# Scores and y on four 64x64 TensorE tiles from chunk 3 on, in a windowed attention followed by a maxout FFN

## Chip, cores and metric

The kernel runs on one core of one Trainium2 chip. The metric is the device time of one execution in microseconds. Engines: TensorE (PE, with its weight loads as PEld), VectorE (DVE), ScalarE (ACT), GpSimd (POOL), and SyncE (SP), which here only issues DMAs.

## The reference

Attention with a causal window of 128 keys and 4 sink keys that every query sees, over 4 batches, 8 heads, 768 positions and head size 64; its output, with heads side by side, goes through a feed-forward layer that takes the largest of three projections (512 to 768) and projects back.

```python
scores = scale * np.matmul(q, k.transpose(0, 1, 3, 2))
is_sink = pos[None, :] < n_sink
in_window = (rel >= 0) & (rel < window)      # rel = query position - key position
scores = np.where(is_sink | in_window, scores, -1e9)
a = softmax(scores)
x = np.matmul(a, v)                          # then (B*S, H*D) = (3072, 512)
h = np.maximum(np.maximum(x @ w1, x @ w2), x @ w3)
out = h @ w_out
```

Inputs and output are float32; the kernel multiplies in bfloat16 and sums in float32.

## The kernel before

The 3072 rows are cut into 12 chunks of 256, three per batch (CPB = 3). A chunk has two blocks of 128 positions, and position 2p+i of the chunk is stored as partition p with i beside it, so a block is 64 partitions by i = 0, 1. Chunks pass through stages whose order is written out by hand for every engine (`manual_schedule`): a long list for chunks 0 to 3 (L486 to L692), then a loop over i = 3..11 (L693) in which chunk n = i + 1 does its attention, chunk i the first FFN product and chunk m = i - 1 the second.

- `load` (L76) issues the DMAs of q, k and v from SP. Some are gated by a small POOL instruction that writes into their target first (L469, L473), which sets when SP may issue them.
- `cast_qk` (L95) and `cast_v` (L104) cast to bfloat16, in the loop on POOL: two casts for k, two for q, four for v (64 partitions each, into `vb`).
- q and k are transposed to head size by position (`qT`, `kT`): for early chunks on TensorE (`turn`, L109, `turn2`), from chunk 4 on by DMA transposes that SP issues (`turn_dma`, L150): one DMA for q, two for k (64 source partitions each).
- `sink_k`, `sink_v` (L224, L310), once per batch: POOL copies the sink keys out of `kT` to `ks`; TensorE picks the sink values with the selector `sel` into `sv`, DVE casts them to `vs`.
- `score` (L259): for a pair p of heads, head a sits in row half a of TensorE (64 rows each). The keys of a block are the stationary operand, 64x128, so two tiles, one per head, run side by side. Each head's 128x512 PSUM bank `st` takes [last block of the chunk before x first query block | own first block x both | own second block x second]. The first chunk of a batch leaves out the first part (128x384).
- `expo` (L282), ACT: exponential from PSUM to `e_sb`. `mask` (L289), DVE: product with a 0/1 mask `msk` (or `msk0` in a batch's first chunk, which lets the sink keys through). The masks are made at the start (`masks`, `factors`).
- `sink_score` (L294): scores against the sink keys, four column tiles of 128x32 (`sk`), and their exponential.
- `av_open`, `av` (L324, L339): product with v; a column of ones gives the sum, and DVE divides (`rc`, `x_sb`).
- `xpose_dma` (L375), SP: a DMA transpose of x to `xT`.
- `ffn_h` (L383): three products per pair of output blocks (864 matmuls of 128x256 in all); ACT copies the first from PSUM, DVE takes the maximum with the others.
- y = h @ w_out: for chunks 4 to 10 of the loop in `y_turn` (L422), two turns of twelve 64x128 matmuls between the score groups. In turn 0, row half a of the contraction adds to bank a, in turn 1 to the other, so the two row halves never write one bank together; a small matmul, the fence, guards the bank. Else `ffn_y` (L406) with full tiles.

The PSUM has eight banks, which the program hands out by a list (`bank`, `give`). In a pass i of the loop between the first and the last two, TensorE's order is: sink scores, scores of pairs 0 and 3, y turn 0, scores of pairs 1 and 2, y turn 1, `av_open`, `av` between groups of `ffn_h`. SP's order in a pass is: q transpose of chunk i+2, loads of chunk i+3, k transposes of chunk i+2, x transpose of chunk i+1, store of chunk i-1.

Of the kernel before, what the change touches and what calls it, by code (L numbers as in the profile page):

```python
# [16 lines left out]
def kernel(  # L17
# [31 lines left out]
    with tc.manual_schedule():  # L49
# [16 lines left out]

        RING = 4
# [6 lines left out]
        raws, bfs = {}, {}  # L74

# [28 lines left out]
        def cast_v(ci, n, i, eng):  # L104
            eng.tensor_copy(  # L105
                vb[ci % RING][64 * i:64 * i + 64, n, :, 0:D],
                raws[ci, "v"][64 * n:64 * n + 64, :, i])

        def turn(ci, w, g, eng=None):  # L109
# [8 lines left out]
            if w == "q":  # L118
                f(  # L119
                    qT[ci % RING][:, 2 * g:2 * g + 2].rearrange("q p i n r -> q (p i) (n r)"), pt)  # L120
            else:
# [28 lines left out]
        def turn_dma(ci, w):  # L150
# [7 lines left out]
            for n in range(2):  # L158
                nc.sync.dma_start_transpose(
                    out=kT[ci % RING][:, n].rearrange("q p i r -> q (p i) r"),  # L160
                    in_=bfs[ci, w][64 * n:64 * n + 64].rearrange("q p i a d -> q (p i a d)"))
# [27 lines left out]
        msk0 = const.tile([128, 2, 3, 128], BF16, name="msk0")  # L189

# [20 lines left out]

        sel = const.tile([128, 2, 32], BF16, name="sel")

# [10 lines left out]
        def sink_k(b):  # L224
            x = kT[(b * CPB) % RING]
# [33 lines left out]
        def score(ci, pairs):  # L259
            b, c = divmod(ci, CPB)  # L260
# [20 lines left out]

        def expo(ci, p):  # L282
            lo = 0 if ci % CPB else 1
# [5 lines left out]
        def mask(ci, p, eng=None):  # L289
            lo = 0 if ci % CPB else 1  # L290
# [3 lines left out]
        def sink_score(ci):  # L294
# [4 lines left out]
            for p in range(NP):  # L299
                nc.tensor.matmul(  # L300
                    st[32 * p:32 * p + 32].rearrange("q n (i r) -> q n i r", i=2),
                    lhsT=ks[b % 2][:, p],
                    rhs=qT[ci % RING][:, p].rearrange("q i n r -> q n i r"),
                    start=True, stop=True, tile_position=(0, 32 * p))
# [5 lines left out]
        def sink_v(b):  # L310
# [3 lines left out]
            for a in range(2):  # L314
                for p in range(NP):
                    nc.tensor.matmul(
                        sv[32 * p:32 * p + 32, a], lhsT=sel[:, a], rhs=x[:, 0, 2 * p + a],
# [21 lines left out]
        def av(ci, p):  # L339
# [16 lines left out]
            if ci not in xs:  # L356
                xs[ci] = work.tile([128, 2, NP, 2, D], BF16, tag="x", bufs=2, name="x_sb")
            nc.vector.tensor_mul(xs[ci][:, :, p], o[:, :, :, 0:D],  # L358
# [5 lines left out]
        def xpose(ci, t, eng=None):  # L364
            eng = eng or nc.scalar
            if t == 0:
                xTs[ci] = work.tile([128, 2, DS, 128], BF16, tag="xT", bufs=3, name="xT")
            pt = bank([128, DS, 128], BF16, "xt")
            x = xs[ci][:, t].rearrange("q p a d -> q (p a d)")
            for ds in range(DS):  # L370
                nc.tensor.transpose(pt[:, ds], x[:, ds * 128:(ds + 1) * 128], ident)
            (nc.scalar.copy if eng is nc.scalar else eng.tensor_copy)(xTs[ci][:, t], pt)
            give(pt)

        def xpose_dma(ci, eng=None):  # L375
            xTs[ci] = work.tile([128, 2, DS, 128], BF16, tag="xT", bufs=3, name="xT")
            (eng or nc.sync).dma_start_transpose(
                out=xTs[ci].rearrange("q t s r -> q (t s) r"),
                in_=xs[ci].rearrange("q t p a d -> q (t p a d)"))
# [3 lines left out]
        def ffn_h(ci, fp, wi, cuts=1, eng=nc.scalar):  # L383
# [3 lines left out]
            for f in range(2):  # L387
                c0 = (2 * fp + f) * 128
                for ds in range(DS):
                    nc.tensor.matmul(  # L390
                        hp[:, f].rearrange("q (i t r) -> q i t r", i=2, t=2),
                        lhsT=w_sb[wi][:, ds, c0:c0 + 128],
                        rhs=xTs[ci][:, :, ds].rearrange("q t (i r) -> q i t r", i=2),
# [28 lines left out]
        def y_turn(ci, turn):  # L422
# [3 lines left out]

            for fb in range(FB):
                for a in range(2):
                    t = a ^ turn
                    hp = slice(64 * a, 64 * a + 64)  # L430
                    nc.tensor.matmul(  # L431
# [420 lines left out]
```

## Time and profile before

| | |
|---|---|
| median of 3 runs | 177.1 us (176.81 to 177.53) |
| the profiled execution | 178.83 us, of which the span of its instructions 177.1 us |
| TensorE clock granted | 1.00 |
| DMA | 34.91 MB, mean 197 GB/s |

The span is counted from the first instruction of the program to the last. Rows of the timeline give start and length in us, the engine, the line of the kernel, the operation with its output and inputs, the tile of TensorE (contraction rows * output columns), the shape, and how many instructions are merged. A matmul's length contains its way through the array, so what a matmul costs in a stream is the distance between starts. Rows grouped by line give the busy time and the mean length in ns, then the idle time just ahead and what ended it. Rows of SPq are DMA issues; their length is SP's time, and the data land later.

### The profile page before, as it was taken

To read this page: it belongs to the slowest core of one execution; us is meant where nothing else is said; L and a number is where in the kernel's file an instruction comes from. 1 tells how busy PE (TensorE), PEld (TensorE's weight loads), DVE (VectorE), ACT (ScalarE), POOL (GpSimd) and SP (SyncE) were. 2 spreads that over 40 slices of the span, in tenths; PEclk is the share of its full clock that TensorE was granted. 3 is DMA by queue.
4 is the path that set the end of the run, shared out by engine and by line. 5 is a ranking of instruction groups with operands and counts; after the bars stand their busy time and mean duration, and the time that the engine had idled before them with its cause. 6 is when DMAs were issued, how large, how long until landed. Compare 5 with 4: busy or idle time off the path is not lost.

```text
span 177.1 us, 4816 instructions
## 1 busy us (share of the span) xinstructions
PE 167.9 (95%) x1956; PEld 128.2 (72%) x1961; DVE 121.7 (69%) x263; ACT 86.8 (49%) x174; POOL 65.9 (37%) x126
## 2 busy tenths in 40 slices
PE   7869988899999999999999999999999999999992
PEld 2436777676688588598698797697797796796871
DVE  3287763679599696677776775876776776876451
ACT  4588525477871931931823914914715716420210
POOL 7289605454685296056055046065073000000000
PEclk9999999999999999999999999999999999999999
DMA  5999999999999999799998999997999405303203
GB/s 144 298 282 181 161 223 236 222 288 276 277 197 302 289 229 237 172 301 171 229 262 214 230 217 234 183 273 194 255 210 226 73 15 162 122 0 63 118 2 118
DMA packets 70694, 34.91 MB, mean 197 GB/s; under 512 B 26640, under 2 KB 69136, under 8 KB 70672
## 3 DMA queue, kind: packets, MB, share of 16 engines
q1 hardware_dynamic: 64976, 31.33, 79.4%
q0 software_dynamic: 5552, 3.15, 12.9%
q8 instruction: 15, 0.25, 0.6%
q10 hardware_dynamic: 144, 0.13, 0.2%
q14 instruction: 7, 0.06, 0.1%
HBM read 25.17 MB, written 6.29 MB: 178 GB/s over the span
## 4 chain that ended last, share of the span: by engine, by line
PE 75%; DMA 11%; POOL 6%; DVE 5%; issue 2%; POOLq 0%; SPq 0%; DVEq 0%
PE h_ps L390 44%; PE y_ps L431 10%; DMA q_raw<-in_q_dram 7%; PE y_ps L411 6%; PE st L274 5%; PE o L350 5%; DMA v_raw<-in_v_dram 3%; POOL w L237 3%; DVE h_sb L401 2%; POOL vb L105 1%; PE o L332 1%; DVE e_sb L292 1%; PE y_ps L453 1%; DVE x_sb L358 1%; PE pt L115 1%
## 5 line engine op out<-in xcount | busy, mean ns | idle before, releaser
L390 PE MATMUL h_ps<-xT,w 128*128 128x256 bf16 x864 | 101.6, 273 | 0.9 <-DMA w<-in_moe_w_dram 0.8
L390 PEld LDWEIGHTS <-w 128*128 128x128 bf16 x864 | 81.6, 98 | 11.8 <-DMA w<-in_moe_w_dram 1.2
L401 DVE TENSOR_TENSOR h_sb<-h_sb,h_ps 128x512 bf16<-128x512 bf16 (+1 forms) x74 | 49.1, 670 | 19.7 <-PE h_ps L390 18.0
L286 ACT ACTIVATE e_sb<-st 128x512 bf16<-128x512 f32 (+1 forms) x96 | 45.9, 585 | 6.6 <-PE st L274 6.5
L397 ACT CAST h_sb<-h_ps 128x512 bf16<-128x512 f32 x35 | 20.6, 589 | 49.7 <-PE h_ps L390 49.6
L292 DVE TENSOR_TENSOR e_sb<-e_sb,msk 128x1024 bf16<-128x1024 bf16 (+1 forms) x42 | 28.0, 679 | 10.8 <-ACT e_sb L286 10.8
L105 POOL CAST vb<-v_raw 64x512 bf16<-64x512 f32 x42 | 27.8, 661 | 15.7 <-DMA v_raw<-in_v_dram 13.2
L101 POOL CAST k_bf<-k_raw 128x512 bf16<-128x512 f32 x18 | 11.0, 630 | 40.0 <-DMA k_raw<-in_k_dram 32.8
L358 DVE TENSOR_TENSOR x_sb<-o,rc 128x256 bf16<-128x256 f32 x48 | 20.4, 424 | 1.6
L431 PE MATMUL y_ps<-wo,h_sb 64*128 64x512 bf16 x168 | 20.7, 376 | 0.0
L350 PE MATMUL o<-vb,e_sb 128*128 128x65 bf16 x352 | 16.6, 193 | 0.8 <-ACT e_sb L286 0.8
L350 PEld LDWEIGHTS <-e_sb 128*128 128x128 bf16 x352 | 14.6, 97 | 3.2 <-ACT e_sb L286 1.0
L274 PE MATMUL st<-qT,kT 64*128 64x128 bf16 (+1 forms) x256 | 14.8, 237 | 0.2 <-DVE qT L119 0.2
L101 POOL CAST q_bf<-q_raw 128x512 bf16<-128x512 f32 x17 | 10.2, 619 | 9.0 <-DMA q_raw<-in_q_dram 9.0
L274 PEld LDWEIGHTS <-kT 64*128 64x128 bf16 x256 | 9.2, 94 | 5.6 <-issue 1.8
L431 PEld LDWEIGHTS <-h_sb 64*128 64x128 bf16 x168 | 8.9, 94 | 5.7
L411 PE MATMUL y_ps<-wo,h_sb 128*128 128x512 bf16 x49 | 12.6, 380 | 0.3
L355 DVE RECIPROCAL rc<-o 128x4 f32<-128x4 f32 x48 | 8.4, 174 | 3.6 <-PE o L350 3.6
L306 ACT ACTIVATE e_sink<-sk 128x256 bf16<-128x256 f32 x8 | 3.1, 389 | 13.3 <-PE sk L300 13.3
L411 PEld LDWEIGHTS <-h_sb 128*128 128x128 bf16 x54 | 4.9, 98 | 5.4 <-DVE h_sb L401 0.5
L237 POOL DMA_DIRECT2D w<-in_moe_w_dram x9 | 7.1, 790 | 0.0
L445 DVE COPY y_sb<-y_ps 128x512 f32<-128x512 f32 x8 | 5.4, 686 | 0.8 <-PE y_ps L431 0.5
(73 smaller groups left out, 87.3 us busy)
## 6 DMA issues: line engine op xcount, KB each, us to landing
k_raw<-in_k_dram SPq DMA_DIRECT2D x11, 512.0 KB, 5.5
v_raw<-in_v_dram SPq DMA_DIRECT2D x11, 512.0 KB, 7.5
out_dram<-y_sb SPq DMA_DIRECT2D x11, 512.0 KB, 3.1
q_raw<-in_q_dram SPq DMA_DIRECT2D x10, 512.0 KB, 7.2
w<-in_moe_w_dram POOLq DMA_DIRECT2D x9, 256.0 KB, 6.8
q_raw<-in_q_dram SPq DMA_DIRECT2D x4, 256.0 KB, 8.5
wo<-in_moe_w_out_dram POOLq DMA_DIRECT2D x2, 384.0 KB, 8.2
v_raw<-in_v_dram SPq DMA_DIRECT2D x2, 256.0 KB, 5.9
```

What stands on the lines that cost most here:

```text
L101: f(x[:, 2 * g:2 * g + 2].rearrange("q p i a d -> q p a i d"), y[:, 4 * g:4 * g + 4].rearrange("q (p a) i d -> q p a i d", a=2))
L105: eng.tensor_copy(vb[ci % RING][64 * i:64 * i + 64, n, :, 0:D], raws[ci, "v"][64 * n:64 * n + 64, :, i])
L274: nc.tensor.matmul(st[a][:, s:s + q1 - q0].rearrange("q n (i r) -> q n i r", i=2), lhsT=x[hp, n, p].rearrange("q i r -> q (i r)"), rhs=qc[ ...
L286: nc.scalar.activation(e[:, a, lo:], st[a][:, lo:], AF.Exp, scale=scale)
L292: (eng or nc.vector).tensor_mul(e[:, :, lo:], e[:, :, lo:], msk0 if lo else msk)
L350: nc.tensor.matmul(o[:, t, a], lhsT=e[:, a, s], rhs=vb[cv % RING][:, n, 2 * p + a], start=first, stop=True, skip_group_check=True)
L358: nc.vector.tensor_mul(xs[ci][:, :, p], o[:, :, :, 0:D], rc.unsqueeze(3).to_broadcast([128, 2, 2, D]))
L390: nc.tensor.matmul(hp[:, f].rearrange("q (i t r) -> q i t r", i=2, t=2), lhsT=w_sb[wi][:, ds, c0:c0 + 128], rhs=xTs[ci][:, :, ds].rearrang ...
L397: (nc.scalar.copy if eng is nc.scalar else eng.tensor_copy)(dst, hp)
L401: nc.vector.tensor_max(dst[:, x], dst[:, x], hp[:, x])
L411: nc.tensor.matmul(yp, lhsT=hs[ci][:, fb, t * 128:(t + 1) * 128], rhs=wo[:, fb], start=(fb == 0), stop=(fb == FB - 1))
L431: nc.tensor.matmul(yps[ci][t], lhsT=hs[ci][hp, fb, t * 128:(t + 1) * 128], rhs=wo[hp, fb], start=(turn == 0 and fb == 0), stop=(turn == 1 ...
```

## The change

From chunk 3 on (NEW = 3):

- Scores (`score4`): a key block is cut into halves h of 64 keys, which are the halves of its positions and not of its parity. Head a and half h make four 64x64 tiles: row half a, and output partitions 64h to 64h+63 of the bank. Each half meets only the quarters (64 positions) of the queries that it can see, so a bank takes 6 quarters, 128x384, in a chunk with a predecessor. In the lower half the step over the own first block streams four quarters, and the last of them is overwritten by the next step.
- For this the keys lie in `kT` by quarters of 32 partitions (`quarters`), queries and all that follows in the order (quarter, i, r). `turn_dma` transposes k by four DMAs of 32 source partitions each. `cast_v` makes two casts of 32 partitions each for one of 64 (in the loop eight for four). `ffn_h` reads xT in runs of 32 elements, so that its output has the order of before.
- `expo4` writes 128x384 per head to `e_part`; `mask4` reads `e_part` with an overlapping pattern, multiplies by the new mask `msk2` and writes the full 128x1024 `e_sb` that `av` reads as before.
- The masks are new: `masks2` on POOL in place of the second `factors` (L592), `masks3` on POOL ahead of `cast_v(4, 1, 0)` (L662). `sel2` selects the sink values for batches 1 to 3.
- `y_turn`: 64x64 tiles as well, 24 matmuls a turn for 12.
- x and `xT` keep their sizes with two dimensions exchanged.

```diff
         def cast_v(ci, n, i, eng):
...
+            for h in range(2):
+                x, y = 64 * h + 32 * i, 64 * n + 32 * h
+                eng.tensor_copy(
+                    vb[ci % RING][x:x + 32, n, :, 0:D], raws[ci, "v"][y:y + 32, :, i])
...
-            for n in range(2):
+            for j in range(4):
                 nc.sync.dma_start_transpose(
-                    out=kT[ci % RING][:, n].rearrange("q p i r -> q (p i) r"),
-                    in_=bfs[ci, w][64 * n:64 * n + 64].rearrange("q p i a d -> q (p i a d)"))
+                    out=quarters(ci)[:, j].rearrange("q p i r -> q (p i) r"),
+                    in_=bfs[ci, w][32 * j:32 * j + 32].rearrange("q p i a d -> q (p i a d)"))
...
+        def masks2():
+            nc.gpsimd.memset(keep, 1.0)
+            for h in range(2):
+                for i in range(2):
+                    hp = slice(64 * h + 32 * i, 64 * h + 32 * i + 32)
+                    nc.gpsimd.affine_select(
+                        out=keep[hp, 0], in_=keep[hp, 0], compare_op=ALU.is_gt, fill=0.0,
+                        base=64 * h + i, pattern=[[-64, 2], [-1, 2], [-2, 32]],
+                        channel_multiplier=2)
+                    nc.gpsimd.affine_select(
+                        out=keep[hp, 1], in_=keep[hp, 1], compare_op=ALU.is_ge, fill=0.0,
+                        base=-64 * h - i, pattern=[[64, 2], [1, 2], [2, 32]],
+                        channel_multiplier=-2)
+            nc.gpsimd.tensor_copy(msk0[:, :, 1:3], keep.unsqueeze(1).to_broadcast([128, 2, 2, 128]))
+            nc.gpsimd.tensor_copy(msk0[:, :, 0], keep[:, 1:2].to_broadcast([128, 2, 128]))
+            for i in range(2):
+                nc.gpsimd.memset(msk0[32 * i:32 * i + 2, :, 0:2], 1.0)
...
+        def masks3():
+            nc.gpsimd.tensor_copy(msk2, keep.unsqueeze(1).to_broadcast([128, 4, 2, 128]))
...
+        def score4(ci, pairs):
...
+            if c:
+                steps = (((kp, 1, 0, 1, 0), (kc, 0, 0, 4, 1), (kc, 1, 2, 4, 4)),
+                         ((kp, 1, 0, 2, 0), (kc, 0, 1, 4, 2), (kc, 1, 3, 4, 5)))
+            else:
+                steps = (((kc, 0, 0, 4, 0), (kc, 1, 2, 4, 4)),) * 2
+            for p in pairs:
+                st = [bank([128, 6, 64], F32, "st") for a in range(2)]
+                for s in range(len(steps[0])):
+                    for h in range(2):
+                        x, n, q0, q1, at = steps[h][s]
+                        for a in range(2):
+                            hp = slice(64 * a, 64 * a + 64)
+                            nc.tensor.matmul(
+                                st[a][64 * h:64 * h + 64, at:at + q1 - q0]
+                                    .rearrange("q j (i r) -> q j i r", i=2),
+                                lhsT=x[hp, 2 * n + h, p].rearrange("q i r -> q (i r)"),
+                                rhs=qT[ci % RING][hp, p].rearrange("q i n r -> q i (n r)")
+                                    .rearrange("q i (j r) -> q j i r", r=32)[:, q0:q1],
+                                start=True, stop=True)
...
             for fb in range(FB):
-                for a in range(2):
...
+                for h in range(2):
+                    for a in range(2):
+                        t = a ^ turn
+                        hp = slice(64 * a, 64 * a + 64)
+                        c = t * 128 + 64 * h
+                        nc.tensor.matmul(
+                            yps[ci][t][64 * h:64 * h + 64], lhsT=hs[ci][hp, fb, c:c + 64],
+                            rhs=wo[hp, fb], start=(turn == 0 and fb == 0),
+                            stop=(turn == 1 and fb == FB - 1), skip_group_check=True)
...
-        factors(msk0, addm0)
+        masks2()
...
         ffn_h(2, 0, 0)
+        masks3()
         cast_v(4, 1, 0, nc.gpsimd)
```

More of the change, by code (lines that the diff above doesn't have):

```diff
@@ L356, in av @@
             if ci not in xs:
[L357 to L358 removed]
+                xs[ci] = work.tile([128, NP, 2, 2, D], BF16, tag="x", bufs=2, name="x_sb")
+            nc.vector.tensor_mul(xs[ci][:, p], o[:, :, :, 0:D],
                                  rc.unsqueeze(3).to_broadcast([128, 2, 2, D]))
```

105 lines of the change are left out of this document (80 added, 25 removed).

## Prediction

> **What bounds the kernel now.** I read the page first (busy time, slices, chain), then TensorE in order of time in one pass of the loop, then POOL and SP around its start.
>
> ```profile
> PE 167.9 (95%) x1956; PEld 128.2 (72%) x1961; DVE 121.7 (69%) x263; ACT 86.8 (49%) x174; POOL 65.9 (37%) x126
> ...
> PE 75%; DMA 11%; POOL 6%; DVE 5%; issue 2%; POOLq 0%; SPq 0%; DVEq 0%
> ```
>
> TensorE is busy 95% of the span and carries 75% of the chain. One pass of the loop, chunk i = 4, from TensorE's timeline, and the busy time of this pass and the next (last columns: granted clock, DMA share, GB/s):
>
> ```profile
> 70.68 0.29 PE L300 MATMUL sk<-qT,ks 128*32 128x256 bf16 x4
> 70.91 0.62 PE L274 MATMUL st<-qT,kT 64*128 64x128 bf16 x12
> 71.36 1.46 PE L431 MATMUL y_ps<-wo,h_sb 64*128 64x512 bf16 x12
> 72.66 0.22 PE L274 MATMUL st<-qT,kT 64*128 64x128 bf16 x1
> ...
> 73.13 1.47 PE L431 MATMUL y_ps<-wo,h_sb 64*128 64x512 bf16 x12
> ```
> ```profile
> 70.75:83.76 13.01, 13.01 (x168) 10.22 (x169) 9.46 (x19) 6.57 (x13) 5.18 (x10) 1.00 1.01 209
> 83.76:95.93 12.17, 12.17 (x146) 9.53 (x149) 9.01 (x19) 5.52 (x12) 3.69 (x7) 1.00 1.18 228
> ```
>
> TensorE is busy 13.01 of 13.01 us, DVE 9.46, ACT 6.57, POOL 5.18. Whatever shortens TensorE's own work is gained, and whatever makes it wait in order is lost in full. The DMA share of 1 and more says that what feeds it has little to spare.
>
> **The change, part by part.**
>
> *Scores (gain).* Twelve y matmuls last from 71.36 to 72.66: six rounds of two, 0.216 us per round of 512 columns, 0.42 ns a column. A pair of heads in a chunk with a predecessor streams 128+256+128 = 512 columns per row half: two pairs 1024, 0.43 us; measured 71.36 - 70.91 = 0.45. After, the lower key half streams 64+256+128 = 448 columns and the upper 128+192+64 = 384. With four tiles side by side the longer one sets the time: 64 columns fewer, 27 ns a pair. Only chunks 4, 5, 7, 8, 10 and 11 have that, 24 pairs: **-0.65 us**. Chunks 3, 6 and 9 stream 256+128 = 384 before and after: 0. No 64x64 tile runs in this trace; the nearest rows are the column tiles of sv and sk:
>
> ```profile
> 56.89 0.25 PE L316 MATMUL sv<-vb,sel 128*32 128x65 bf16 x8
> 56.96 0.28 PE L300 MATMUL sk<-qT,ks 128*32 128x256 bf16 x4
> 57.18 0.62 PE L274 MATMUL st<-qT,kT 64*128 64x128 bf16 x12
> ```
>
> Eight matmuls of 65 columns take 0.07 us up to the next start, two rounds of 0.035; one after the other 65 columns alone need 8 x 27 ns = 0.22. So four column tiles do run side by side, with 8 ns a round that streaming doesn't cover, which I put down to weight loads. One such exposure per pair, at its 64-column matmuls, is 24 x 8 ns = 0.2: I take **-0.45** (ends -0.65, and 0 if all four loads of a round queue: 0.035/4 = 9 ns for 32 columns, 18 for 64, twelve of them 0.21, as long as a pair now).
>
> *y in 64x64 tiles.* 24 matmuls a turn for 12, still six rounds of 512 columns: **0**; without four at a time it doubles (third rival). The drain at a change of tile shape (0.22 us from sk to st, where 256 columns stream in 0.11) occurs as often as before: 0. The L390 matmuls read xT in runs of 32 elements for 64; no row shows such a read. I take 0; each per cent would cost 0.01 x 101.6 x 9/12 = 0.76 (groups below).
>
> ```profile
> L390 PE MATMUL h_ps<-xT,w 128*128 128x256 bf16 x864 | 101.6, 273 | 0.9 <-DMA w<-in_moe_w_dram 0.8
> ...
> L105 POOL CAST vb<-v_raw 64x512 bf16<-64x512 f32 x42 | 27.8, 661 | 15.7 <-DMA v_raw<-in_v_dram 13.2
> L292 DVE TENSOR_TENSOR e_sb<-e_sb,msk 128x1024 bf16<-128x1024 bf16 x30 | 21.1, 716 | 7.7 <-ACT e_sb L286 7.7
> ...
> L195 POOL TENSOR_SCALAR_AFFINE_SELECT addm<-addm 64x128 bf16<-64x128 bf16 x2 | 0.6, 293 | 0.1
> ```
>
> *ACT and DVE in the loop.* Eight exponentials a pass shrink from 512 to 384 elements; ACT is busy 6.57 of 13.0 and I see no wait on it to shorten: 0 (but see the fourth rival). The mask keeps 1024 elements (716 ns) but reads overlapping runs; at double the price DVE has 9.46 + 4 x 0.7 = 12.3 of 13.0, still covered: 0.
>
> *POOL in the loop.* Casts of v are split into 32 partitions: eight for four. The time goes by elements per partition, not partitions (661 ns at 64, above), so +2.6 us on 5.18 of 13: covered, 0.
>
> *POOL ahead of the loop.* masks2 takes the place of two L210 (1.07): eight selects at 293, memsets and copies, by these rows some 5 us, so +4.
>
> ```profile
> 31.06 1.07 POOL L210 TENSOR_SCALAR msk<-addm 128x384 bf16<-128x384 bf16 x2
> 34.53 1.26 POOL L105 CAST vb<-v_raw 64x512 bf16<-64x512 f32 x2 [2.40 <-DMA v_raw<-in_v_dram]
> ...
> 40.20 0.73 POOL L101 CAST q_bf<-q_raw 128x512 bf16<-128x512 f32 x1 [2.32 <-DMA q_raw<-in_q_dram]
> ...
> 44.27 1.93 POOL L105 CAST vb<-v_raw 64x512 bf16<-64x512 f32 x3
> 47.21 0.84 POOL L101 CAST k_bf<-k_raw 128x512 bf16<-128x512 f32 x1 [1.01 <-DMA k_raw<-in_k_dram]
> ...
> 50.24 2.50 POOL L105 CAST vb<-v_raw 64x512 bf16<-64x512 f32 x3
> 52.69 0.71 POOL L228 COPY ks<-kT 64x16 bf16<-64x16 bf16 x2
> ```
>
> POOL idles 2.40 and 2.32 us here for data: masks2 is swallowed by 40.20, at 0. What follows is not. From 44.27: six casts for three (3.9) end at 48.1; the cast of k (0.84) at 49.0, +0.95; masks3, 1024 elements by 0.53 us for 384 some 1.3, at 50.3; two casts (1.5) and a gate at 51.9; six more at 0.83 (2.50 for three) at 56.9; ks (0.71) at **57.6**. The sink scores read ks at 56.96: TensorE stands in order, **+0.6**. Behind them in the queue stand chunk 4's scores and y of chunk 2, for which ACT and DVE wait. One cast of v on DVE is split too; at POOL's 0.66 that puts 0.7 us on DVE just ahead, beside this wait and not on top: 0.
>
> *SP.* Each chunk's k is transposed by four DMAs of 32 partitions for two of 64. By line: all k issues (shortest, median, longest in ns), the time to landing of q's, and SP in order of time:
>
> ```profile
> L159 SPq DMA_TRANSPOSE kT<-k_bf x16: 1193/1534/4177, 48.1 to 137.3; - x16
> ```
> ```profile
> DMA to landing us min/median/max: 3.2/3.9/5.5
> ```
> ```profile
> 48.08 3.93 SPq L159 DMA_TRANSPOSE kT<-k_bf  x2
> 52.07 1.30 SPq L154 DMA_TRANSPOSE qT<-q_bf  x1
> ...
> 60.42 5.34 SPq L159 DMA_TRANSPOSE kT<-k_bf  x2
> 65.86 1.26 SPq L154 DMA_TRANSPOSE qT<-q_bf  x1
> ...
> 74.55 4.08 SPq L159 DMA_TRANSPOSE kT<-k_bf  x2
> 80.87 1.23 SPq L377 DMA_TRANSPOSE xT<-x_sb  x1
> ```
>
> At least, an issue costs 1.19 us for 64 partitions (k), and about as much for 128 (q 1.26, x 1.23): it doesn't follow the partitions. I take 1.2 for 32 (lower end 0.6, by halving): +2.4 us of SP per chunk, less what SP now waits for room in the queue. Chunk 4: k from 49.0, q at 54.0 (+2.0), landing 3.2 later at 57.2, behind ks. Chunk 5: all behind it 2.0 late; 5.34 becomes about 7.0 (two more issues, and 0.7 less wait for room, an estimate: a piece half as large needs half the room); q goes at 65.86 + 2.0 + 1.65 = 69.5 and lands at 72.7. TensorE wants it for the sink scores at 70.68 + 0.6 = 71.3, with chunk 5's scores and the first turn of y behind them: **+1.4**. Later passes: k ends at 78.63 and SP waits until 80.87, 2.2 us of room; xT lands some 3.2 later, 84.1, and is read after two score groups and two turns of y, 2 x (0.45 + 1.30) past 83.76, so has 3.2 us in hand: 0 (second rival if not).
>
> *The rest* (layouts of x and xT, the sink scores' order of columns, sel2) keeps the number and size of the instructions: 0.
>
> *Sum:* -0.45 + 0.6 + 1.4 = **+1.55**. The profiled execution took 178.83 us (span 177.1), so it would take 180.4. The median of the runs is 177.1 (176.81 to 177.53); on it the sum gives **178.6**.
>
> **Rivals.**
> 1. *Not slower: a piece is cheap to issue.* If 32 partitions cost 0.6 us, four cost SP what two cost now, q for chunk 5 goes as early as before, and only ks is late: -0.45 + 0.6, **177.3**. It decides below about 0.75 us a piece. For it: fewer rows to describe. Against: 64 and 128 cost the same.
> 2. *SP becomes the bound of the loop.* Its round is 13.0 less 2.2 of waiting, 10.8; plus 2.4, 13.2, where passes take 13.0 and 12.2. That is 0.2 late in four passes and 1.0 in the two short ones: +2.8 on the forecast, **181.4**. For it: DMA shares above 1, so transposes may land later still. Against: room won back, and what xT has in hand.
> 3. *The four tiles don't run together.* Two at a time, the 14 turns of y double (14 x 1.30 = 18.2) and scores take 832 columns for 512 (0.13 x 24) and 768 for 384 (0.16 x 12), 5.0: +23, **200**. Against: sv above. The Trainium skill, "TensorEngine Tiling (Array Packing)", section Restrictions, says that column tiling disables fast weight loads, and its page "TensorE: Matmul & The Clock Gate", section on LDWEIGHTS, gives P / 1.2 ns for P columns: 53 ns here; by that, an estimate, twelve loads in a row make a pair 0.64 us and the total about 190. No row here shows a 64-column load; the 32-column round of 0.035 us speaks against loads in a row.
> 4. *The waits are swallowed and the gain is whole.* POOL's casts at 0.64 instead of 0.83 end ks 1.1 sooner, before it is wanted, and SP goes as in rival 1. The second score group lasts 73.13 - 72.66 = 0.47, 0.02 longer than the first; if that is a wait for banks, shorter exponentials end it: 14 x 0.02. -0.65 - 0.28, **176.2**. For it: DVE's work beside POOL, which may set the 0.83, doesn't grow. Against: both waits must go.
>
> **How the numbers follow.** Forecast 0.42 (178.0 to 179.6), rival 1 0.22, rival 2 0.13, rival 3 0.06, rival 4 0.17. A measurement of this kernel can tell about 0.5% from no change, 176.2 to 178.0. Slower: the forecast, 2 and 3, 0.61. Within: rival 1 and half of 4, 0.30. Faster: the other half, 0.09. The range leaves out rival 3, that half of rival 4, and a slower read of xT on top of rival 2: **176.2 to 181.5**.
>
> **What would show it.** Right: ks ending near 57.6 and sk starting after it; four kT issues near 1.2 us each; qT of chunk 5 landing after TensorE is ready; st of two pairs 0.40 us in the loop; y turns of 1.30. Wrong: kT issues of 0.6; turns near 2.6; L390 matmuls starting farther apart than before; waits of TensorE for kT or xT in later passes.

## The result, and the profile after

The changed kernel takes **187.6 us** (median of 6 runs, 186.52 to 188.47), the kernel before 177.08 beside it: 1.058 times as long, interval 1.054 to 1.063, or 10.5 us more. The prediction was 178.6 with a range of 176.2 to 181.5. The sign was right, the size was not. The profiled execution after took 188.15 us with a span of 186.4. The ratios below leave out runs more than 1.5% above the fastest of the same kernel: two of e3's four (186.2 and 186.5 us), one of e10's, three of e15's four (194.2 to 195.0) and one of the kernel before.

The page of the changed kernel: busy time, and the chain that ended last.

```profile
PE 172.1 (92%) x2321; PEld 131.4 (70%) x2321; DVE 126.9 (68%) x264; ACT 82.9 (44%) x174; POOL 98.0 (53%) x176
...
PE 44%; DMA 29%; POOL 16%; SPq 6%; issue 3%; ACT 0%; DVE 0%; POOLq 0%
```

TensorE carried 75% of the chain before and carries 44% now; DMA went from 11% to 29%, and SP's queue, 0% before, has 6%. Something that TensorE waits for has become the bound. Its waits (us in total, times, longest), first two rows:

```profile
PE st L349 <- DMA kT<-k_bf: 3.8, 5, 0.9
PE sk L415 <- DMA qT<-q_bf: 2.4, 1, 2.4
```

Neither wait existed before. In TensorE's timeline the second stands at the start of pass i = 4, and the first, again and again, in later passes:

```profile
72.45 0.29 PE L415 MATMUL sk<-qT,ks 128*32 128x256 bf16 x4 [2.40 <-DMA qT<-q_bf]
...
73.04 2.51 PE L552 MATMUL y_ps<-wo,h_sb 64*64 64x512 bf16 x24
75.25 0.31 PE L349 MATMUL st<-qT,kT 64*64 64x128 bf16 x1
```
```profile
100.82 0.39 PE L349 MATMUL st<-qT,kT 64*64 64x64 bf16 x14 [0.94 <-DMA kT<-k_bf]
...
116.08 0.39 PE L349 MATMUL st<-qT,kT 64*64 64x64 bf16 x14 [0.66 <-DMA kT<-k_bf]
```

The first turn of y behind the 2.40 us wait lasts from 73.04 to 75.25, 2.2 us instead of 1.30. The busy time of that whole pass, with the granted clock in the third column from the end:

```profile
72.45:87.00 14.55, 14.55 (x214) 11.71 (x214) 9.11 (x18) 5.90 (x13) 9.32 (x14) 0.88 0.88 183
```

14.55 us of work without a gap where the pass had 13.0, at a clock of 0.88: behind the wait TensorE ran slower for a while.

SP in the round that makes pass i = 6 late (from one q transpose to the next), then all issues of kT (shortest, median, longest in ns):

```profile
88.04 1.30 SPq L173 DMA_TRANSPOSE qT<-q_bf  x1
89.40 0.76 SPq L99 DMA_DIRECT2D k_raw<-in_k_dram  x1
90.20 0.63 SPq L99 DMA_DIRECT2D q_raw<-in_q_dram  x1
90.88 1.55 SPq L99 DMA_DIRECT2D v_raw<-in_v_dram  x1
92.48 7.21 SPq L178 DMA_TRANSPOSE kT<-k_bf  x4
99.78 1.25 SPq L490 DMA_TRANSPOSE xT<-x_sb  x1
101.13 0.54 SPq L580 DMA_DIRECT2D out_dram<-y_sb  x1
101.75 2.70 SPq L173 DMA_TRANSPOSE qT<-q_bf  x1
```
```profile
L178 SPq DMA_TRANSPOSE kT<-k_bf x32: 1186/1252/2530, 47.3 to 151.2; - x32
```

In this round SP hardly idles: the pieces take 7.21 us, where two took 3.8 to 5.5 before, and the 0.7 to 2.2 us in which it used to wait for x ahead of the xT transpose are gone. From one xT issue to the next it now takes 13.1 to 15.3 us (71.31, 84.45, 99.78, 114.99, 128.99, 143.12) where it took 12.3 to 13.0.

What to measure the runs by: the **loop stretch**, from the first sink-score matmul of chunk 5 (L415, 72.45 here) to the one-column fence matmul of pass i = 10 (L558, 158.69) in TensorE's timeline. It is 78.66 us before and 86.24 after, +7.6. Of these, 1.5 are the first pass at the lower clock, 4.0 are time in which TensorE stands still (3.8 of it for kT), and 2.0 are matmul groups that count as busy but last longer. The two profiled executions differ by 9.3 us in their spans: 7.6 in the loop, 1.8 in its later start (72.45 for 70.68; TensorE was ready 0.6 sooner and then waited 2.40), and nothing behind it.

### The profile page after: what moved, and what is told of

It is laid out like the page before. It is cut to its first block, busy times and chain, and to the rows that moved or that the text cites. A ratio compares the mean times of both kernels' runs of the same rounds, so it can differ in the third digit from the quotient of the medians.

```text
span 186.4 us, 5623 instructions
## 1 busy us (share of the span) xinstructions
PE 172.1 (92%) x2321; PEld 131.4 (70%) x2321; DVE 126.9 (68%) x264; ACT 82.9 (44%) x174; POOL 98.0 (53%) x176
## 4 chain that ended last, share of the span: by engine, by line
PE 44%; DMA 29%; POOL 16%; SPq 6%; issue 3%; ACT 0%; DVE 0%; POOLq 0%
PE h_ps L509 27%; DMA q_raw<-in_q_dram 9%; POOL vb L121 8%; PE y_ps L552 8%; DMA v_raw<-in_v_dram 7%; DMA kT<-k_bf 5%; DMA w<-in_moe_w_dram 3%; SPq L99 3%; PE st L349 3%; PE o L463 3%; DMA k_raw<-in_k_dram 3%; PE y_ps L529 2%; DMA qT<-q_bf 2%; POOL w L285 2%; POOL k_bf L110 1%
## 5 line engine op out<-in xcount | busy, mean ns | idle before, releaser
L121 POOL CAST vb<-v_raw 32x512 bf16<-32x512 f32 x70 | 49.4, 706 | 13.2 <-DMA v_raw<-in_v_dram 10.4
L381 DVE TENSOR_TENSOR e_sb<-e_part,msk 128x1024 bf16<-128x1024 bf16 x24 | 18.6, 796 | 12.5 <-ACT e_part L366 12.3
L366 ACT ACTIVATE e_part<-st 128x384 bf16<-128x384 f32 x48 | 19.7, 498 | 6.2 <-PE st L349 6.1
L552 PE MATMUL y_ps<-wo,h_sb 64*64 64x512 bf16 x336 | 22.2, 395 | 0.0
L349 PE MATMUL st<-qT,kT 64*64 64x128 bf16 (+3 forms) x384 | 13.5, 238 | 4.0 <-DMA kT<-k_bf 3.8
L349 PEld LDWEIGHTS <-kT 64*64 64x64 bf16 x384 | 9.0, 109 | 9.2 <-DMA kT<-k_bf 5.5
L552 PEld LDWEIGHTS <-h_sb 64*64 64x64 bf16 x336 | 10.8, 112 | 4.9 <-issue 0.3
L366 ACT ACTIVATE e_sb<-st 128x384 bf16<-128x384 f32 x24 | 9.9, 498 | 5.9 <-PE st L349 5.9
L390 ACT ACTIVATE e_sb<-st 128x512 bf16<-128x512 f32 (+1 forms) x24 | 11.6, 588 | 2.0 <-PE st L324 1.9
L372 DVE TENSOR_TENSOR e_sb<-e_sb,msk 128x768 bf16<-128x768 bf16 x12 | 7.4, 622 | 3.3 <-ACT e_sb L366 3.3
```

Of the source, the lines that this page charges most:

```text
L121: eng.tensor_copy(vb[ci % RING][x:x + 32, n, :, 0:D], raws[ci, "v"][y:y + 32, :, i])
L349: nc.tensor.matmul(st[a][64 * h:64 * h + 64, at:at + q1 - q0] .rearrange("q j (i r) -> q j i r", i=2), lhsT=x[hp, 2 * n + h, p].rearrange( ...
L366: nc.scalar.activation(dst, st[a], AF.Exp, scale=scale)
L381: nc.vector.tensor_mul(x.rearrange("q a (t s) c -> q (a t) s c", t=2), y, msk2)
L552: nc.tensor.matmul(yps[ci][t][64 * h:64 * h + 64], lhsT=hs[ci][hp, fb, c:c + 64], rhs=wo[hp, fb], start=(turn == 0 and fb == 0), stop=(tur ...
```

## The experiments

Theory 1: the four k transposes per chunk make SP, at 1.2 us an issue, the bound of the loop, and the rest of the change is nearly free. Rival: POOL's doubled casts of v, the masks, or the 64x64 tiles. All runs, each compared with the kernel before run beside it (0.01 in the ratio is 1.77 us):

| run | kernel | ratio (interval) | loop stretch, us |
|---|---|---|---|
| after | as changed | 1.058 (1.054 to 1.063) | 86.24 |
| e1 | after, two k transposes | 1.006 (1.003 to 1.009) | 78.65 |
| e2 | before, four k transposes | 1.042 (1.036 to 1.048) | 83.07 |
| e3 | after, three k transposes | 1.031 (1.026 to 1.035) | 82.95 |
| e4 | before, split casts of v | 1.004 (0.999 to 1.008) | 78.67 |
| e5 | after, filler in the first wait | 1.058 (1.055 to 1.062) | 86.13 |
| e6 | e1, y on 64x128 | 1.017 (1.014 to 1.021) | 80.17 |
| e7 | after, one k transpose, scores 64x32 | 1.020 (1.015 to 1.025) | 81.14 |
| e8 | e1, whole casts of v | 1.004 (1.002 to 1.006) | 78.66 |
| e9 | after, loads issued by ACT | 1.050 (1.046 to 1.053) | 83.34 |
| e10 | after, two of four pieces from ACT | 1.171 (1.167 to 1.175) | 105.70 |
| e11 | before, k in four by columns | 1.037 (1.034 to 1.040) | 82.17 |
| e12 | e7, y on 64x32 too | 1.036 (1.032 to 1.040) | 82.99 |
| e13 | after, loads between pieces | 1.033 (1.027 to 1.039) | 81.49 |
| e14 | before, two tiny transposes more | 1.044 (1.040 to 1.048) | 84.30 |
| e15 | after, pieces before loads | 191.2 us, one run | 88.65 |
| e16 | e13, first pass too | 1.014 (1.009 to 1.019) | 80.23 |
| e17 | before, in e16's order | 0.998 (0.995 to 1.001) | 78.66 |

### Which part of the change it is

**e1**, undoing the split of k alone:

```
-            for j in range(4):
-                nc.sync.dma_start_transpose(out=quarters(ci)[:, j]..., in_=bfs[ci, w][32 * j:32 * j + 32]...)
+            for n in range(2):
+                nc.sync.dma_start_transpose(out=kT[ci % RING][:, n]..., in_=bfs[ci, w][64 * n:64 * n + 64]...)
```

> The changed kernel, but k is transposed by two DMAs of 64 partitions per chunk, as before the change; the keys then land in the old order while the scores, the masks and the casts of v count on the new one, so the output is of other keys (part changed: which key meets which mask and value; the amount of work stays). Theory 1 (four issues per chunk make SP the bound of the loop): SP's round from one xT issue to the next falls from 14 to 15 us to 12.3 to 13.1 as before, the waits of TensorE for kT and for q of chunk 5 go, 176.3 to 178 us. Rival (the split casts of v on POOL, the masks or the 64x64 tiles carry the loss): 184 us or more.

178.41 us, 0.4 above theory 1's range and far from the rival's, and a loop stretch of 78.65 against 78.66 before. So 9.2 of the 10.5 us go with the split of k, and with two pieces the tiles, masks and casts together make no difference in the loop, for better or worse. SP idles ahead of xT again: its kT block ends at 90.72 (86.92 + 3.80) and xT goes at 92.24.

```profile
86.92 3.80 SPq L178 DMA_TRANSPOSE kT<-k_bf  x2
92.24 1.23 SPq L490 DMA_TRANSPOSE xT<-x_sb  x1
```

What e1 has above the kernel before, 1.1 us (0.6 to 1.6), lies outside the loop. Behind it both profiled executions take 27.8 us, so it should lie ahead; the profiles can't show where, because the profiled execution of the kernel before is itself 1.7 us above its median.

**e2**, the converse, splits k in the kernel before into four pieces with the same destinations:

```
-            for n in range(2):
-                ... out=kT[ci % RING][:, n]..., in_=bfs[ci, w][64 * n:64 * n + 64]...
+            for j in range(4):
+                n, h = divmod(j, 2)
+                ... out=kT[ci % RING][:, n, :, :, 32 * h:32 * h + 32]..., in_=bfs[ci, w][32 * j:32 * j + 32]...
```

> The kernel before, with nothing changed but that k is transposed by four DMAs of 32 partitions per chunk into the same places. Theory 1: the whole loss comes with it, and so do the late q of chunk 5 and the waits for kT in later passes: 185 to 188 us. Rival (casts, masks, tiles): at most the late q of chunk 5, 177 to 179.

185.14 us, 8 of the 10.5: the split alone, without any other part of the change, makes most of the loss. The rest of the change isn't free beside four pieces, though: the changed kernel's loop is 3.2 us longer than e2's (86.24 for 83.07), and no run separates which part does that.

**e4** and **e8** take POOL: e4 splits the casts of v in the kernel before (`for h in range(2)` over 32 partitions), e8 makes them whole in e1.

> The kernel before, with nothing changed but that from chunk 3 on each cast of v is two of 32 partitions. Theory 1: POOL's busy time goes from 66 to some 90 us and the time stays, 176.8 to 178.0. Rival (POOL's doubled casts hold k and v back and carry the loss): 181 us or more.

> The run with two k transposes per chunk, but with the casts of v of 64 partitions as before (keys and values out of the order that the masks count on, as in that run; the amount of work stays but for the casts). That run was 1.1 us (0.6 to 1.6) above the kernel before. If the split casts ahead of the loop make it: 177.2 to 177.8. If the new masks on POOL or the tiles do: 178.2 to 178.6.

e4 took 177.84 and e8 177.70, with the loop as before (78.67, 78.66), although POOL's busy time is 91.8 us in e4 for 65.9. Beside two pieces the casts cost nothing in the loop. e8's 177.70 lies in the range forecast for the case that the casts make e1's 1.1 us ahead of the loop, but that is not settled: the intervals of e1 and e8 overlap.

### What the tiles are worth

**e6** is e1 with `y_turn` and the fence as before the change, 64x128.

> The run with two k transposes per chunk, but with y on 64x128 tiles as before, beside scores on 64x64 tiles (the same keys out of order as in that run). If a change of tile width between scores and y costs time, as the change supposes, 0.3 us or more slower than that run (178.4). By my step (drain at each change of tile shape the same, turns of 1.30 either way): 178.2 to 178.5.

179.85, +1.4 on e1, and a loop stretch 1.5 longer, so the first of the two forecasts held. One pass in TensorE's timeline, e1 first, then e6:

```profile
108.35 0.58 PE L349 MATMUL st<-qT,kT 64*64 64x64 bf16 x24
108.72 1.51 PE L552 MATMUL y_ps<-wo,h_sb 64*64 64x512 bf16 x24
110.02 0.22 PE L349 MATMUL st<-qT,kT 64*64 64x128 bf16 x1
```
```profile
111.03 0.58 PE L349 MATMUL st<-qT,kT 64*64 64x64 bf16 x24
111.54 1.47 PE L550 MATMUL y_ps<-wo,h_sb 64*128 64x512 bf16 x12
112.85 0.16 PE L556 MATMUL fence<-wo,h_sb 64*128 64x1 bf16 x1
112.95 0.58 PE L349 MATMUL st<-qT,kT 64*64 64x64 bf16 x24
```

From scores to y it takes 0.37 us in one tile shape and 0.51 with a change of it; back from y to scores 0 and 0.10. The second group takes 0.52 (110.02 to 110.54) and, with the way back in it, 0.61 (112.85 to 113.46), so a pass costs some 0.23 more, which over the loop makes the 1.5. A turn of y is 1.30 in both. So the change's second half (y beside the scores in the same tiles) does save what the first half alone would have cost. The Trainium skill, "TensorEngine Tiling (Array Packing)", section Key Properties, says that changing the tiling mode, not just the tile, drains TensorE; the 0.14 and 0.10 us are this case's price for it. The scores themselves went from 0.45 (prediction, 70.91 to 71.36) to 0.37 in the first group of a pass, and from 0.47 to 0.52 in the second: 0.03 a pass, nothing that the total shows. Why the second group got no shorter stays open.

**e7** and **e12** look for a form that needs no split of k: scores on 64x32 tiles, each with a run of 32 keys of one parity, so that one transpose of 128 partitions does; e12 has y on 64x32 tiles too.

```
-                nc.sync.dma_start_transpose(out=quarters(ci)[:, j]..., ...)      x4
+            nc.sync.dma_start_transpose(out=whole(ci)..., in_=bfs[ci, w]...)
...
-                                lhsT=x[hp, 2 * n + h, p].rearrange("q i r -> q (i r)"),
+                                lhsT=x[hp, p, i, r0:r0 + 32], ... tile_position=(64 * a, c0)
```

> The changed kernel with scores on eight 64x32 tiles, each reading a run of 32 keys of one parity, so that k of a chunk can be transposed by one DMA of 128 partitions as q is. Theory 1: SP is relieved of three issues of 1.2 us per chunk and the loss is gone, 175.5 to 178; if twice as many score matmuls cost 9 ns each (the eight sv matmuls of 32 columns took 0.07 us), a pair of heads takes 0.22 and nothing is lost by them. Rival (casts, masks, y tiles): 184 us or more.

> The run with one transpose of k per chunk and scores on 64x32 tiles took 180.9; here y (and the one-column fence matmul) is on 64x32 tiles too, 48 matmuls a turn. If that run's loss is the change of tile shape between scores and y (0.14 us from scores to y and 0.09 back, four times a pass, as its timeline shows), it goes: 178.0 to 179.0. If eight tiles of y don't run side by side, a turn of y takes over 1.30 us and the total is above 182.

Both missed: 180.93 and 183.89. In e7 SP is relieved and no wait for kT is left; from the first scores of a pass to y it takes 0.52 (96.07 to 96.59; e1 takes 0.42 in that pass, 95.22 to 95.64), the change of shape again. In e12 this is gone (0.40, 110.70 to 111.10, then a turn of 1.30 on eight tiles), but other time appears:

```profile
100.98 0.41 PE L556 MATMUL y_ps<-wo,h_sb 64*32 64x512 bf16 x8 [1.39 <-issue]
```

In the middle of a turn TensorE stands still for 1.39 us with "issue" as the reason, that is for nothing that the profile shows. It stands still 1.40 us more at 142.20, which the profile puts down to an ACT copy that had ended 0.9 us earlier. e12 moves 24 packets on the instruction queue where the kernel before moved 15. That these stalls are the fetch of twice as many instructions is argued, not shown.

### What an issue costs, and to whom

**e11** cuts k of the kernel before into four by columns, not partitions (`n, p = j // 2, 2 * (j % 2)`, 64 partitions by 512). **e14** leaves k as before and adds, per chunk, two transposes of one 32x128 block that nothing reads:

```
+            for n in range(2):
+                nc.sync.dma_start_transpose(out=spare[:, n], in_=bfs[ci, w][64 * n:64 * n + 32, 0, 0]...)
```

> The kernel before with k transposed by four DMAs of 64 partitions and half the columns (two of four head pairs) each, into the same places. Separates what an issue costs: if it is 1.2 us for each DMA whatever its size, this is the run with four pieces of 32 partitions again, 184.5 to 186; if it goes by columns, a piece costs 0.6 us, SP's time is as before, and the total 177 to 178.

> The kernel before with two transposes of one block of 32 partitions by 128 columns per chunk, which nothing reads, behind k's two. If issues in SP's queue make the loss whatever they move, 1.2 us each, 183.5 to 186 as with k by columns (183.8). If a block of 128 columns for 1024 issues in a fraction of that, or if the loss comes from waiting for four pieces of kT instead of two, 177 to 179.

Issue times (shortest, median, longest, ns) in e11 and in e14:

```profile
L160 SPq DMA_TRANSPOSE kT<-k_bf x32: 1182/1247/2515, 46.0 to 147.0; - x32
```
```profile
L164 SPq DMA_TRANSPOSE spare<-k_bf x16: 1212/1224/2227, 48.9 to 149.6; - x16
```

e11 takes 183.82 us, 0.7 below its first range and far above its second. An issue costs 1.2 us whether it moves 128x1024 elements (q, 1.26), 32x1024, 64x512 or 32x128. And e14 takes 185.18 us, as long as e2: two issues that move next to nothing and that nobody waits for make the whole loss of four pieces. It is the added issues themselves that cost, not the data and not the waiting for four pieces.

**e3**, three transposes per chunk (32, 32 and 64 partitions), gives the dose.

> The changed kernel with three transposes of k per chunk: 32, 32 and 64 partitions (the second key block's keys then lie out of the order that masks and scores count on; the amount of work stays). Two gave 178.4 and four 187.6. If a round of SP with two has 1.3 to 2.2 us of waiting to spend, the third issue of 1.2 us fits and only the first pass's q is late by some 0.6: 178.5 to 180. If each small piece costs in proportion (its transfer, not SP's time): 183.

1.031, some 182.4 us from two runs: the third issue costs about 4.3 us and the fourth 4.9 (by the loop stretch 4.3 and 3.3). I had expected the third to fit into SP's 1.3 to 2.2 us of waiting; it doesn't. So "SP's sum of issue times against the pass" is too simple, and the next runs are about that.

**e9** has ACT's queue issue the loop's loads (`load(i + 3, eng=nc.scalar)`), which takes 2.6 us a round and more off SP.

> The changed kernel, four k transposes per chunk from SP as there, but from the loop's second pass on the loads of k, q and v are issued by ACT's queue. Theory 1 (SP's issue time and the room behind it): SP's round loses 2.6 to 2.8 us and falls to 12.5 to 13, TensorE no longer waits for kT in passes 6 to 9, 178.5 to 181 (the first pass's wait for q and its lower clock, 3.3 us, may stay: their issues stand ahead of these loads). Rival (the small transposes themselves are slow on the DMA engines, or land behind the loads whoever issues them): 185 or more. A loss on ACT, whose queue now waits for room too, would show as waits of TensorE for ACT.

186.02: only 1.6 us came back. In the loop stretch it is 2.9 of 7.6, and about half of that is the clock, which stayed at 1.00 in this execution's first pass (13.0 us from its sink scores to the next scores, 14.55 in the changed kernel). The plain form of theory 1, that SP's time alone makes the loss, fell here. SP does wait again (its four pieces end at 82.79, xT goes at 84.86), but pieces issued by 82.79 let TensorE go on only at 89.22:

```profile
76.78 6.01 SPq L178 DMA_TRANSPOSE kT<-k_bf  x4
84.86 1.23 SPq L490 DMA_TRANSPOSE xT<-x_sb  x1
```
```profile
89.22 0.41 PE L349 MATMUL st<-qT,kT 64*64 64x128 bf16 x10 [1.19 <-DMA kT<-k_bf]
```

ACT issues its loads at 78.70 to 81.42, among these pieces. That the loads hold the pieces up is argued, not shown. And because they now go out beside the pieces, the run doesn't tell what SP's time cost in the changed kernel.

**e10** has ACT issue every second piece instead (`eng if eng and j % 2 else nc.sync`).

> The changed kernel with its four pieces, but in the loop from the second pass on every second one is issued by ACT's queue. The transfers stay the same and each keeps its place behind the loads; SP has two issues of 1.2 us less a pass. If SP's issue time makes the loss, SP idles ahead of xT again and passes 6 to 9 lose their waits for kT: 180 to 183 (the first pass stays 2.4 late). If the four small transfers themselves do: 186 or more.

207.76, which tells nothing on theory 1, because the program changed in another way. SP, then ACT's queue:

```profile
77.41 4.78 SPq L178 DMA_TRANSPOSE kT<-k_bf  x2
88.69 1.23 SPq L490 DMA_TRANSPOSE xT<-x_sb  x1
```
```profile
84.87 2.58 ACTq L178 DMA_TRANSPOSE kT<-k_bf  x2
```

SP's pieces, issued by 82.19, landed at 84.54, and only then ACT's go, at 84.87; ACT's landed at 88.55, and only then SP's xT goes, at 88.69. Here the transposes of two queues follow one another. The Trainium skill, "DMA: Bandwidth & Descriptors", section DMA Transpose (X-bar), gives the reason: transposes in flight from two queues can corrupt each other, so programs have to wait in between.

**e5** fills the 2.40 us wait with ten matmuls that nothing reads (`if i == 4: warm(10)` ahead of the sink scores).

> The changed kernel with ten matmuls of 512 columns that nothing reads, put into TensorE's queue ahead of chunk 5's sink scores, where it waited 2.40 us for q. If the wait itself drops the granted clock and so costs another 1.5 us in the pass behind it (14.55 us for 13.01), the clock stays at 1.0 there, that pass takes 13.0 to 13.2 and the whole 1.3 to 1.6 less than the changed kernel, 186.0 to 186.4. If the longer pass has another cause (banks, late kT), pass and time stay, 187.6.

The clock stays up, the turn of y behind it takes 1.30 again (73.32 to 74.62) and the pass 12.98 (to the scores at 85.71), both as forecast, yet the total is 187.18 with the same ratio as the changed kernel. In the profiled execution the time comes back as a longer wait four passes on, with a slow turn of y behind that one:

```profile
72.73 0.29 PE L415 MATMUL sk<-qT,ks 128*32 128x256 bf16 x4 [0.34 <-DMA qT<-q_bf]
...
73.32 1.51 PE L552 MATMUL y_ps<-wo,h_sb 64*64 64x512 bf16 x24
74.62 0.22 PE L349 MATMUL st<-qT,kT 64*64 64x128 bf16 x1
```
```profile
130.13 0.64 PE L349 MATMUL st<-qT,kT 64*64 64x128 bf16 x10 [2.79 <-DMA kT<-k_bf]
130.45 2.87 PE L552 MATMUL y_ps<-wo,h_sb 64*64 64x512 bf16 x24
```

The three other runs have a mean clock of 0.996 to 0.998, against 0.990 and 0.991 for the changed kernel, and take 186.45 to 187.21 all the same. In the changed kernel TensorE's own time isn't what sets the end: what it gains, it waits.

### The order in the queue

Theory 1b: SP issues three loads of 512 KB, then four pieces, xT, the store and the next q, some 12 us in which no load goes out (92.4 to 104.5 in the round above); the DMA engines run dry, and the next loads, with kT behind them in the queue, land late. **e13** puts the loads between the pieces, from the second pass on; **e15** puts the pieces ahead of the loads; **e16** is e13 with the same order in the pass i = 3, and **e17** gives e16's order to the kernel before. The forecasts below are those of e13, e15, e16 and e17, in this order.

```
-                load(i + 3)
...
-                turn_dma(i + 2, 'k')
+                for w, js in (('k', (0, 1)), ('q', (2, 3)), ('v', ())):
+                    load(i + 3, w)
+                    turn_dma(i + 2, 'k', js)
```

> The changed kernel; in the loop from the second pass on SP issues the load of k, two pieces of kT, the load of q, two pieces, the load of v, where it issued three loads and then four pieces. Theory 1b (SP's four issues of 1.2 us in a row, with xT's behind them, let the DMA engines run dry, and the loads that follow make up for it too late): a load of about 2 us now runs beside each two issues, SP's round falls to about 13.2, TensorE's waits for kT after the first pass shrink below 2 us in all, 180 to 183. Plain theory 1 (only the sum of SP's issue times counts): the order changes nothing, 186.5 to 188.

> The changed kernel; in the loop from the second pass on SP issues the four pieces of kT ahead of the three loads, not behind them. If kT is late because it lands behind v's load, it now lands some 5 us sooner and TensorE never waits for it; the loads go 4.8 us later and have most of a pass in hand: 179.5 to 183. If SP's round or the dry DMA engines are the bound, its sum is the same and only what is late changes (xT, q or the casts): 186 or more.

> The run with loads between the pieces, and in the pass ahead of it (i = 3) SP too issues the load of k, two pieces, the load of q, two pieces, the transpose of q, and only then the load of v, for which it had stalled 3.4 us. Theory 1b: q of chunk 5 lands near 68 instead of 73, TensorE (ready at 70) doesn't wait, the clock stays, and the total comes down to the run with two pieces per chunk, 178.4, or up to 1 us above. If four issues cost something that no order hides: 180.5 or more.

> The kernel before with the same order of SP's queue (its two pieces of kT between the loads, in the first pass too). TensorE is busy 95% of its span and has no wait in the loop, so the order is worth nothing there: 176.6 to 177.6. If it gains 0.5% or more, the kernel before was held by its queue as well.

e13 took 182.93 and e16 **179.97**, with the same four pieces and the same issues in another order. e13 is as forecast; e16 lies between its two forecasts (up to 179.4, or 180.5 and more). SP in one round of e13, and TensorE's wait for kT in e13, 3.8 in the changed kernel:

```profile
89.22 0.56 SPq L99 DMA_DIRECT2D k_raw<-in_k_dram  x1
89.84 3.14 SPq L178 DMA_TRANSPOSE kT<-k_bf  x2
93.02 0.58 SPq L99 DMA_DIRECT2D q_raw<-in_q_dram  x1
93.71 3.21 SPq L178 DMA_TRANSPOSE kT<-k_bf  x2
96.97 0.57 SPq L99 DMA_DIRECT2D v_raw<-in_v_dram  x1
```
```profile
PE st L349 <- DMA kT<-k_bf: 0.2, 1, 0.2
```

The pieces still take 6.4 us; the loads' issues shrink from 2.9 us to 1.7, kT no longer stands behind v's load, and the longest stretch without a load is 5.5 us (97.5 to the next round's k at 103.0). The rate of all DMA in the 40 slices, the changed kernel first, then e16:

```profile
GB/s 155 297 269 196 224 215 260 268 266 296 189 129 309 292 93 227 235 202 114 244 253 116 190 295 71 236 297 91 210 287 121 236 43 105 96 90 56 118 0 113
```
```profile
GB/s 147 294 282 197 221 215 260 228 281 287 291 82 261 274 171 153 286 162 197 293 170 226 240 215 200 302 204 206 250 211 191 220 33 178 114 7 59 122 1 118
```

From the 15th to the 31st slice the changed kernel falls to 71 to 121 GB/s once in every pass; e16 doesn't go below 153 there. That is the dry stretch, and the order of issues closes it. It isn't the whole cost of an added issue: e3's slowest slice there is 154 and its loop is still 4.3 us longer than before, and e9 (slowest slice 110, twice) loses 4.7. The new order also changes two things at once, because it feeds the DMA engines and takes part of the loads from ahead of kT; which of the two gives how much is not separated. In e16 the wait for q in the first pass is gone too, and with it the lower clock in the first turn of y (70.75 to 72.05, 1.30). e17 shows that the order is worth nothing where SP has time: 0.998.

e15 went as its second theory had it: 191.2 us, because xT now stands behind the loads. It is issued at 99.86, as in the changed kernel (99.78), but lands 8.9 us later, not 3.2, and TensorE waits for it:

```profile
108.81 3.60 PE L509 MATMUL h_ps<-xT,w 128*128 128x256 bf16 x16 [4.29 <-DMA xT<-x_sb]
```

No version beats the kernel before, and with e1's loop equal to it none was in sight: the scores gain nothing that the total shows. e16 is 7.6 us faster than the changed kernel and still 2.5 slower than before; of these, e1's 1.1 are outside the loop, and 1.6 in it (80.23 for 78.65) remain for four issues that no order tried here hides.

## Why the prediction was wrong

**Sign and first link right.** SP's price was right: 1.2 us a piece whatever its size (1186 ns the shortest). So were the times of chunk 5: q forecast to be issued at 69.5 and to land at 72.7; it was issued at 69.33 and TensorE had it at 72.45. Rival 1 (cheap pieces) is out.

**The step that failed: "Later passes: k ends at 78.63 and SP waits until 80.87, 2.2 us of room; xT lands ... so has 3.2 us in hand: 0".** The loop got 7.6 us longer. The step looked at the slack of xT only. What came late was kT of the next chunk, which stands behind three loads and is wanted at the start of the pass: five waits, 3.8 us. And it took 2.2 us as SP's room, from one round. The other rounds with loads had 1.7, 0.7, 1.7 and 1.5 us between the end of k's issues and xT's, the tightest here:

```profile
100.00 5.49 SPq L159 DMA_TRANSPOSE kT<-k_bf  x2
106.20 1.23 SPq L377 DMA_TRANSPOSE xT<-x_sb  x1
```

Two more issues of 1.2 us don't fit into any of them, and what doesn't fit adds up from pass to pass. That isn't all, because e3 shows that the first added issue already costs 4.3 us. The DMA engines had a share of 1.01 and 1.18 in the windows that the prediction quotes, so an issue that moves little may leave a gap in what feeds them; the order runs fit this, but why one issue costs so much stays open. The prediction wrote "The DMA share of 1 and more says that what feeds it has little to spare" and used it only in favour of rival 2, not in the sum.

**Rival 2** (SP becomes the bound of the loop, 181.4, chance 0.13) had the mechanism. Its size was too small, because it added issue times alone (10.8 + 2.4 = 13.2 us a round) and forecast 2.8 us; the rounds took 13.1 to 15.3. In e16's order they take 12.5 to 13.6 (xT issued at 68.95, 81.53, 94.92, 108.01, 120.50, 134.11): that sum is about what a well-ordered queue gives.

**First pass, +1.4:** q came when forecast, but the wait was 2.40, because TensorE was ready at 70.05 and not at 71.3; half of that is the next term. The lower clock behind it (14.55 us for 13.0) was not foreseen, but e5 shows that it cost nothing by itself here.

**ks, +0.6: wrong.** It was forecast to end at 57.6 and ended at 55.66, ahead of the sink scores at 56.34:

```profile
42.43 4.08 POOL L121 CAST vb<-v_raw 32x512 bf16<-32x512 f32 x6
...
50.28 4.89 POOL L121 CAST vb<-v_raw 32x512 bf16<-32x512 f32 x6
55.23 0.43 POOL L276 COPY ks<-kT 64x16 bf16<-64x16 bf16 x2
```

The six casts at the end took 4.89, 0.82 each as forecast (rival 4 had 0.64), but POOL came to them at 50.28, not 51.9: its work there began at 42.43 instead of 44.27. The two copies took 0.43, not 0.71. How much of the earlier start is only a difference between two executions no run shows. What POOL's new work ahead of the loop costs is within e1's 1.1 us, and not located.

**Scores, -0.45 (ends -0.65 and 0):** it came out at the end 0, as the loop of e1 shows. The prediction's bound by serial loads of 64 columns was 0.21 a pair of heads, 0.42 for two; 0.37 for two pairs is below that, so the loads do overlap in part.

**y in 64x64 tiles, 0: right** (1.30 a turn in e1), so rival 3 is out. So are its loads in a row, for which it gave an estimate of about 190: that is near the measured time by luck, because e1 has the same loads and takes 178.4. **Reading xT in runs of 32: right**, and **ACT, DVE, POOL in the loop, 0: right** beside two pieces, by e1, e4 and e8 (beside four, e2's shorter loop leaves it open). The rows on the profile page after: the products that read xT (273 ns as before), POOL's casts of 32 partitions, and the mask (796 ns for 716):

```profile
L509 PE MATMUL h_ps<-xT,w 128*128 128x256 bf16 x864 | 101.7, 273 | 0.6 <-DMA w<-in_moe_w_dram 0.4
...
L121 POOL CAST vb<-v_raw 32x512 bf16<-32x512 f32 x70 | 49.4, 706 | 13.2 <-DMA v_raw<-in_v_dram 10.4
...
L381 DVE TENSOR_TENSOR e_sb<-e_part,msk 128x1024 bf16<-128x1024 bf16 x24 | 18.6, 796 | 12.5 <-ACT e_part L366 12.3
```

**Rival 4** (both waits swallowed) is out with rival 1.

## What to carry to other kernels

When a change splits a DMA, count issues and not bytes, and look at what stands behind them in the same queue: here, with DMA shares of 1.0 to 1.2 in the loop, an issue that moves little cost more than the queue's spare time suggested. Take that spare time from all rounds, not from one. Before undoing such a split, reorder it: big loads between the small issues, and what is wanted first not behind three loads, gave back 7.6 of 10.5 us here. When a wait of the busiest engine is the result of a late queue, keeping that engine at its full clock gave nothing (e5), so the slack has to be worked out for everything in the queue, not for the one transfer at its end.

## What the runs showed of the hardware

- A DMA transpose within SBUF costs its queue 1.2 us to issue, from 32x128 to 128x1024 elements alike (1.18 to 1.26), and a small one landed 2.3 us after the start of its issue at the least (the shortest in e11 and e14).
- A change of tile shape between matmuls cost TensorE 0.14 us one way and 0.10 the other (64x64 to 64x128 and back, first group of a pass, e6 against e1); eight 64x32 tiles run side by side as four 64x64 do (1.30 us a turn either way).
- With twice as many matmuls in the score and y groups, TensorE stood still for 1.39 us (e12) without a reason in the profile, and for 1.40 behind an ACT copy that had ended 0.9 us earlier.
- The granted clock fell after waits of 1.97 us (e14: 0.58 from 128 to 131), 2.40 (the changed kernel) and 2.79 (e5), and stayed at 1.00 after waits of 2.72 (e14) and 2.83 (e9) for q: length alone doesn't decide.
